# The opening and the hand-over of a fused attention and MLP kernel in another order: ACT's function table, the mixing matrices' loads, the first tile's transposes and scores, three loads of x

## The chip, the cores and the metric

One NeuronCore of a Trainium2 chip runs the whole program. The metric is device time in microseconds (us), the median of several runs. TensorE is called PE, its weight loads PEld, VectorE DVE, ScalarE ACT, GpSimd POOL and SyncE SP. DMAs are issued by SP and, in the opening, by ACT.

## The reference

Four batches, 12 heads, 448 positions, head size 64. Talking-heads attention, whose heads are mixed before and after the softmax, feeds an MLP with a piecewise quadratic gate:

```
scores = q @ k^T / 8                                  # per head, 448 x 448
scores = einsum('bhij,hg->bgij', scores, w_pre)       # mix the 12 heads
attn   = softmax over j of scores
attn   = einsum('bhij,hg->bgij', attn, w_post)        # mix again
x      = (attn @ v) laid out as 1792 x 768
h      = x @ w_in                                     # 768 -> 2048
g      = h where h >= 1, 0 where h <= -1, else (h + 1)^2 / 4
out    = g @ w_out                                    # 2048 -> 768
```

## The kernel before, in words

The order of the work is written out by hand: each engine runs its instructions as the program gives them. The attention has 16 tiles, four per batch (120, 120, 120 and 88 query positions). A tile's steps are:

- `load_q`, `load_k` bring q and k in. k of a batch comes in six head pairs of two heads each. In the first batch the two heads of a pair are two DMAs, one issued by SP and one by ACT (L101).
- `trans_q` (L138 to 141) and `trans_k` (L121 to 128) transpose them on PE into PSUM. ACT then writes a rounded high part (`qh`, `kh`) and DVE the remainder (`ql`, `kl`).
- `scores` (L155) makes the products of two head pairs, 12 matmuls; ACT (L160) and DVE (L164) copy the four results of each call to `ssb`.
- `load_s` (L179) reads ssb back through a DMA on SP, so that 10 positions times 12 heads stand on the partitions: a block.
- `pre` (L185) multiplies a block by `wpre`, which mixes the heads; `row_max` (L189), `exps` (L195) and `norm` (L201 to 206) make the softmax and scale `wpost`; `post` (L216, L218) mixes again; `pv` (L232) multiplies by v.

The blocks are worked off in 48 groups of three or four. In step n of the main loop SP first gets `load_s` for group n + 1. PE then runs `pre` of group n, `post` of group n - 1, and what the tables `at`, `vis2` and `vis` add (transposes, `pv`, scores of later tiles). Last comes the list `late[n]`, filled by `put(n, ...)`: other loads and stores, and near the end the splits of the MLP's operands. NG is 48 and NE is 44. Everything that SP issues stands in one queue; a DMA that must wait holds all DMAs behind it.

Each DMA reports to one of eight semaphores, DMAHW0 to DMAHW7, in turn. The ninth DMA of the program therefore waits on its issuing engine until the first has landed, and so on.

**The opening.** SP issues q of the first tile (in two halves), its half of the k loads and q of the second tile. ACT issues the other half of the k loads and then two small loads of w_pre and w_post (`wrep`, L480). ACT's function table is loaded before its first ACTIVATE (L140). `warm` (L499) issues matmuls whose results nobody reads. PSUM tiles of the tag "q" (two buffers, shared by `warm`, the first transposes of q and half of the scores) and "l" (six buffers) are used in turn.

**The hand-over to the MLP.** In steps 44 to 48 the first 512 rows of x are loaded back from DRAM in six pieces (`load_x`, L382, tile `xr`, three buffers) and split into `xh` on ACT (L390) and `xl` on DVE (L391) by `split_x`. A fourth piece can be loaded only when the first has been split. `load_w` (L353, L355) loads the MLP's weights and `split_w` (L373, L374) splits them; `ffn1` (L404) is the MLP's first matmul.

Of the kernel before, what the change touches and what calls it, by code (L numbers as in the profile page):

```python
# [9 lines left out]
F32 = mybir.dt.float32  # L10
# [4 lines left out]
AF = mybir.ActivationFunctionType  # L15
# [7 lines left out]
def tile_talking_heads_moe(  # L23
# [11 lines left out]
    nc = tc.nc  # L35
    B, H, S, D = q.shape
    NT, DM = out.shape
    DFF = w_in.shape[1]
    HP = H // 2
    HG = HP // 2  # L40
    IB = 10
    KM = IB * H
    QT = 12 * IB
    KC = 4
    KP = S // KC
    KDM = DM // 128
# [6 lines left out]
    const = ctx.enter_context(tc.tile_pool(name="const", bufs=1))  # L53
# [10 lines left out]
    ps_q = s_qk.enter_context(tc.tile_pool(name="ps_q", bufs=2, space=PSUM, side="right"))  # L64
# [8 lines left out]
    for b in range(B):  # L73
        for i0 in range(0, S, QT):
            n = min(QT, S - i0)
            tiles.append((b, i0, n, -(-n // IB)))
    blocks = []
    groups = []
# [17 lines left out]
    def load_k(b, hp, t=None):  # L96
        first = t is not None
        if t is None:
            t = qp.tile([KP, KC, 2, D], F32, tag="kraw", name="kraw", bufs=2)
        for s in range(2):  # L100
            (nc.scalar if first and s else nc.sync).dma_start(out=t[:, :, s, :], in_=k[b, 2 * hp + s].rearrange("(p r) d -> p r d", r=KC))  # L101
        kraw[b, hp] = t

    def load_q(t, gs=(0, 1)):
        b, i0, n, nb = tiles[t]
        if 0 in gs:
            qraw[t] = qp.tile([128, H, D], F32, tag="qraw", name="qraw", bufs=2)
        for g in gs:
            h = slice(g * HP, (g + 1) * HP)
            nc.sync.dma_start(out=qraw[t][:n, h], in_=q[b, h, i0:i0 + n].rearrange("h p d -> p h d"))  # L110
# [5 lines left out]
    def trans_k(b, hp):  # L116
        kt[b, hp] = [qp.tile([128, S], F32R, tag=f"k{c}{hp}", name=f"k{c}{hp}", bufs=1) for c in "hl"]
        x = kraw.pop((b, hp))
        ps = ps_l.tile([128, S], F32, tag="l", name="ps_k")
        for r in range(KC):  # L120
            nc.tensor.transpose(out=ps[:, r * KP:(r + 1) * KP], in_=x[:, r, :, :],  # L121
                                identity=ident[:KP, :KP])
        hi, lo = kt[b, hp]
        if b:
            nc.vector.tensor_copy(out=hi, in_=ps)
        else:
            nc.scalar.activation(out=hi, in_=ps, func=AF.Copy)
        nc.vector.tensor_tensor(out=lo, in0=ps, in1=hi.bitcast(F32), op=ALU.subtract)

    def trans_q(t, g):  # L130
        n = tiles[t][2]
        x = qraw[t]
        if g == 0:
            qt[t] = [qp.tile([128, HP, QT], F32R, tag=f"q{c}", name=f"q{c}") for c in "hl"]
        ps = (ps_l if t > 1 else ps_q).tile([128, HG, QT], F32, tag="l" if t > 1 else "q", name="ps_t")
        for m in range(HG):
            h = 2 * (g * HG + m)
            nc.tensor.transpose(out=ps[:, m, :n], in_=x[:n, h:h + 2, :], identity=ident[:n, :n])  # L138
        hi, lo = (x[:, g * HG:(g + 1) * HG, :n] for x in qt[t])
        nc.scalar.activation(out=hi, in_=ps[:, :, :n], func=AF.Copy)  # L140
        nc.vector.tensor_tensor(out=lo, in0=ps[:, :, :n], in1=hi.bitcast(F32), op=ALU.subtract)

    def scores(t, hps):

        b, i0, n, nb = tiles[t]
        if hps[0] == 0:
            ssb[t] = sp.tile([QT, H, S], F32, tag="ssb", name="ssb")
        todo = []
        rest = []
        for u, hp in enumerate(hps):  # L150
            ps = [(ps_l if u else ps_q).tile([QT, S], F32, tag="l" if u else "q", name=f"ps_s{s}")
                  for s in range(2)]
            for m, (x, y) in enumerate(((0, 0), (1, 0), (0, 1))):
                for s, r in enumerate(half):
                    nc.tensor.matmul(out=ps[s][:n], lhsT=qt[t][x][r, hp, :n], rhs=kt[b, hp][y][r, :],  # L155
                                     start=(m == 0), stop=(m == 2))
            (rest if u else todo).append((2 * hp, ps[0]))
            rest.append((2 * hp + 1, ps[1]))
        for h, x in todo:
            nc.scalar.activation(out=ssb[t][:n, h, :], in_=x[:n], func=AF.Copy)  # L160

        def copies():
            for h, x in rest:
                nc.vector.tensor_copy(out=ssb[t][:n, h, :], in_=x[:n])  # L164
        return copies
# [9 lines left out]
    def load_s(m):  # L175
        t, o, ni, c = blocks[m]
        n, nb = tiles[t][2:]
        x = ap_.tile([KM, S], F32, tag="s10", name="s10", bufs=8)
        nc.sync.dma_start(out=x[:ni * H], in_=ssb[t][o:n:nb])  # L179
        s10[m] = x  # L180
# [168 lines left out]
    def load_w(f):  # L349
        if f not in wraw:  # L350
            alloc_w(f)
        wi, wo = wraw[f]
        nc.sync.dma_start(out=wi, in_=wid[f])  # L353
        if f < NWO:
            nc.sync.dma_start(out=wo, in_=wod[f])  # L355
# [23 lines left out]
    def load_x(j, kk):  # L379
        t0, n = bat[j]  # L380
        x = pool['fp'].tile([128, TB], F32, tag="xr", name="xr", bufs=3)
        nc.sync.dma_start(out=x[:, :n], in_=xd[:, kk, t0:t0 + n])  # L382
        xraw[j, kk] = x

    def split_x(j, kk):
        n = bat[j][1]
        hi = pool['fp'].tile([128, TB], F32R, tag="xh", name="xh", bufs=KDM + 2)
        lo = pool['fp'].tile([128, TB], F32R, tag="xl", name="xl", bufs=KDM + 2)
        src = xraw.pop((j, kk))[:, :n]
        nc.scalar.activation(out=hi[:, :n], in_=src, func=AF.Copy)  # L390
        nc.vector.tensor_tensor(out=lo[:, :n], in0=src, in1=hi[:, :n].bitcast(F32), op=ALU.subtract)  # L391
        xs[j, kk] = (hi, lo)
# [65 lines left out]


    with tc.manual_schedule():  # L460
        load_q(0, (0,))
        k0 = [ap_.tile([KP, 2, KC, 2, D], F32, tag=f"v{g}", name=f"k0{g}", bufs=1) for g in range(3)]
        load_k(0, 0, k0[0][:, 0])
        load_q(0, (1,))
        for hp in range(1, HP):
            load_k(0, hp, k0[hp // 2][:, hp % 2])
        load_q(1)
        ident = const.tile([128, 128], F32, name="ident")
        make_identity(nc, ident)

# [3 lines left out]
                                base=0, pattern=[[-H, IB]], channel_multiplier=1)  # L474
        nc.gpsimd.affine_select(out=mask, in_=mask, compare_op=ALU.is_ge, fill=0.0,
                                base=H - 1, pattern=[[H, IB]], channel_multiplier=-1)
        wrep = const.tile([128, 2, H], F32, name="wrep")
        nc.vector.memset(wrep, 0.0)
        for n, w in enumerate((w_pre, w_post)):
            nc.scalar.dma_start(out=wrep[:KM, n, :], in_=w.unsqueeze(0).to_broadcast([IB, H, H]))  # L480

        wpre = const.tile([128, 128], F32, name="wpre")
        wpost = const.tile([128, H, IB], F32, name="wpost")
# [3 lines left out]
            out=wpre[:, :KM].rearrange("p (i g) -> p i g", g=H),  # L487
# [2 lines left out]
        nc.vector.tensor_tensor(  # L490
            out=wpost, in0=wrep[:, 1, :].unsqueeze(2).to_broadcast([128, H, IB]),
            in1=mask.unsqueeze(1).to_broadcast([128, H, IB]), op=ALU.mult)
        c05 = const.tile([128, 1], F32, name="c05")
        nc.vector.memset(c05, 0.5)

        def warm(n):
            ps = ps_q.tile([128, 128], F32, tag="q", name="ps_w")
            for m in range(n):
                nc.tensor.matmul(out=ps, lhsT=ident, rhs=ident, start=True, stop=True)  # L499

        warm(10)
        trans_q(0, 0)
        trans_k(0, 0)
        trans_q(0, 1)
        for hp in range(1, HP):
            warm(3)
            trans_k(0, hp)
            if hp in (3, 5):
                warm(2)
                scores(0, [hp - 3, hp - 2])()  # L510
        warm(4)
        scores(0, [4, 5])()
        for m in groups[0]:
            load_s(m)
        load_q(2)
        trans_q(1, 0)
        trans_q(1, 1)
# [4 lines left out]
        def put(n, f):  # L522
            late.setdefault(n, []).append(f)
# [18 lines left out]
        for t in range(len(tiles)):  # L542
            for g in range(3):
                w0 = 3 * t + 4 + g if t + 1 < len(tiles) else NG + 1
# [8 lines left out]
        NE = NG - 4  # L553
        for j in range(3):
            put(NE, lambda j=j: load_x(0, j))
        put(NE, lambda: load_w(0))
        for kk in range(KDM):
            put(NE + 1 + kk // 2, lambda kk=kk: split_x(0, kk))
            if kk + 3 < KDM:
                put(NE + 1 + kk // 2, lambda kk=kk: load_x(0, kk + 3))  # L560
        for f in range(1, NWE):
            put(NE + f, lambda f=f: load_w(f))
        put(NG - 1, lambda: split_w(0))
# [6 lines left out]
        for n in range(NG + 2):  # L570
            if n == NE:
# [4 lines left out]
                    name="ps_h", bufs=2, space=PSUM, side="right", reuse_waits="tile"))  # L576
# [29 lines left out]
            for f in [scores(t, hps) for t, hps in vis.pop(n, ())]:  # L606
                f()
# [79 lines left out]
```

## Time and profile before

| What | Value |
|---|---|
| median of three runs | 975.99 us (975.35 to 978.43) |
| the profiled execution, its own time | 973.09 us |
| its span | 971.4 us |
| PE busy | 947.6 us, 98% of the span |
| DVE, ACT, POOL busy | 57%, 53%, 17% |

The profile belongs to one execution. Its times count from the span's start; 1.7 us of its own time lie around the span. A row of the timeline gives start, length, engine, line, operation, `out<-in`, count, and in brackets the idle time of that engine before it with what ended it. An engine's name with a q (ACTq, SPq) is its sequencer issuing a DMA: the length is that of issuing, not of the transfer. An fp32 matmul is recorded as two PE entries, so ten `warm` matmuls are 20 entries.

### The profile page before, as it was taken

How to read it: one execution, taken by the hardware profiler on the slowest of the kernel's cores; microseconds unless marked ns; L12 is line 12 of the kernel's file. 1: busy time of each engine (PE TensorE's matmuls, PEld its weight loads, DVE VectorE, ACT ScalarE, POOL GpSimd, SP SyncE). 2: the span in 40 equal slices, each digit the busy share in tenths (PEclk: the TensorE clock that was granted, in tenths of full speed). 3: DMA queues.
4: the chain of work that ended last, by engine and by line, in shares of the span. 5: the costliest groups of instructions: out<-in, count | busy, mean ns of one | idle time of the engine just before them, and what ended most of it. 6: DMA issues, size and time to landing. Idle time of an engine off the chain costs nothing.

```text
span 971.4 us, 17796 instructions
## 1 busy us (share of the span) xinstructions
PE 947.6 (98%) x6698; PEld 775.7 (80%) x6698; DVE 554.7 (57%) x997; ACT 517.9 (53%) x1097; POOL 169.2 (17%) x253
## 2 busy tenths in 40 slices
PE   7999999999999999999899999999999999999997
PEld 6667777777778787777688877888888888888997
DVE  3665756666665756654355566554454644545774
ACT  2566577666676666665555454443333533334553
POOL 0134233323333233422201212000000000000000
PEclk8999999999999999999999999999999999999999
DMA  5685657775667856653544432020000200000100
GB/s 88 177 240 163 198 177 216 212 211 176 198 199 218 218 173 206 191 196 107 166 163 140 149 128 87 11 98 1 1 23 1 92 1 1 12 1 6 65 2 33
DMA packets 118362, 115.22 MB, mean 119 GB/s; under 512 B 61700, under 2 KB 107268, under 8 KB 118276
## 3 DMA queue, kind: packets, MB, share of 16 engines
q1 hardware_dynamic: 115232, 113.37, 38.4%
q10 hardware_dynamic: 3044, 0.70, 0.5%
q8 instruction: 54, 0.88, 0.4%
q14 instruction: 32, 0.26, 0.1%
HBM read 55.85 MB, written 19.66 MB: 78 GB/s over the span
## 4 chain that ended last, share of the span: by engine, by line
PE 91%; DMA 3%; DVE 2%; ACT 1%; issue 1%; POOL 1%; ACTq 0%; SPq 0%; POOLq 0%
PE o L441 22%; PE ps_h L404 22%; PE ps_l L185 15%; PE ps_a L216 15%; PE ps_x L232 8%; PE ps_s L155 7%; DMA s<-ssb 2%; PE ps_w L499 1%; PE ps_k L121 1%; PE ps_t L138 1%; POOL wo L286 1%; DMA k<-in_k_dram 1%; DMA wi<-wid 0%; DVE mx L418 0%; DVE mx L417 0%
## 5 line engine op out<-in xcount | busy, mean ns | idle before, releaser
L216 PEld LDWEIGHTS ps_a<-wr,e 128*112 128x112 f32 x1440 | 154.6, 177 | 18.5 <-issue 18.5
L195 ACT ACTIVATE e<-ps_l,nm 128x448 f32<-128x448 f32 x180 | 113.0, 632 | 94.3 <-DVE nm L189 93.7
L206 POOL TENSOR_SCALAR wr<-wpost,rs 128x120 f32<-128x120 f32 x180 | 103.2, 591 | 337.1 <-DVE rs L202 290.4
L185 PE MATMUL ps_l<-s,wpre 120*128 120x448 f32 x360 | 150.3, 559 | 6.6 <-DMA s<-ssb 6.6
L216 PE MATMUL ps_a<-wr,e 128*112 128x120 f32 (+1 forms) x1440 | 155.3, 266 | 0.0
L404 PE MATMUL ps_h<-xh,wil 128*128 128x512 f32 (+1 forms) x384 | 139.5, 363 | 0.0
L404 PE MATMUL ps_h<-xl,wih 128*128 128x512 f32 (+1 forms) x384 | 139.2, 363 | 0.0
L404 PE MATMUL ps_h<-xh,wih 128*128 128x512 f32 (+1 forms) x384 | 139.2, 362 | 0.0
L185 PEld LDWEIGHTS ps_l<-s,wpre 120*128 120x128 f32 x360 | 64.6, 191 | 72.2 <-issue 62.0
L441 PE MATMUL o<-woh,gl 128*128 128x512 f32 x448 | 115.7, 339 | 4.4 <-DVE gl L421 4.4
L189 DVE TENSOR_REDUCE nm<-ps_l 128x1 f32<-128x448 f32 x180 | 105.1, 618 | 21.1 <-PE ps_l L185 16.0
L441 PE MATMUL o<-woh,gh 128*128 128x512 f32 x448 | 115.6, 339 | 0.0
L441 PE MATMUL o<-wol,gh 128*128 128x512 f32 x448 | 115.2, 339 | 0.0
L417 DVE TENSOR_TENSOR mx<-ps_h,a 128x512 f32<-128x512 f32 (+1 forms) x64 | 39.9, 624 | 120.6 <-ACT a L416 120.6
L164 DVE COPY ssb<-ps_s 120x448 f32<-120x448 f32 (+1 forms) x144 | 82.6, 619 | 44.3 <-PE ps_s L155 41.4
L416 ACT ACTIVATE a<-ps_h,c 128x512 f32<-128x512 f32 (+1 forms) x64 | 40.5, 633 | 113.5 <-PE ps_h L404 113.4
L218 ACT ACTIVATE aT<-ps_a 112x480 f32<-112x480 f32 x180 | 96.0, 591 | 4.9 <-PE ps_a L216 3.6
L441 PEld LDWEIGHTS o<-woh,gl 128*128 128x128 f32 x448 | 75.1, 189 | 17.9 <-DVE gl L421 6.8
L420 ACT ACTIVATE gh<-mx 128x512 fp32r<-128x512 f32 (+1 forms) x64 | 37.0, 578 | 92.5 <-DVE mx L418 92.5
L441 PEld LDWEIGHTS o<-wol,gh 128*128 128x128 f32 x448 | 76.3, 188 | 10.0
L441 PEld LDWEIGHTS o<-woh,gh 128*128 128x128 f32 x448 | 76.4, 188 | 9.7
L232 PE MATMUL ps_x<-aT,v 112*64 112x120 f32 (+1 forms) x1536 | 83.8, 262 | 0.0
(66 smaller groups left out, 1246.5 us busy)
## 6 DMA issues: line engine op xcount, KB each, us to landing
s<-ssb SPq DMA_DIRECT2D x172, 210.0 KB
wraw<-in_moe_w_in_dram SPq DMA_DIRECT2D x32, 384.0 KB
raw<-in_moe_w_out_dram SPq DMA_DIRECT2D x20, 384.0 KB
wid<-wt SPq DMA_DIRECT2D x32, 192.0 KB
wi<-wid SPq DMA_DIRECT2D x16, 384.0 KB
v<-in_v_dram SPq DMA_DIRECT2D x12, 448.0 KB
out_dram<-osb SPq DMA_DIRECT2D x14, 384.0 KB
wraw<-in_moe_w_out_dram SPq DMA_DIRECT2D x12, 384.0 KB
```

What stands on the lines that cost most here:

```text
L155: nc.tensor.matmul(out=ps[s][:n], lhsT=qt[t][x][r, hp, :n], rhs=kt[b, hp][y][r, :], start=(m == 0), stop=(m == 2))
L164: nc.vector.tensor_copy(out=ssb[t][:n, h, :], in_=x[:n])
L185: nc.tensor.matmul(out=lps[m], lhsT=wpre[:k], rhs=s10.pop(m)[:k], start=True, stop=True)
L189: nc.vector.tensor_reduce(out=nm, in_=lps[m], axis=AX.X, op=ALU.max, negate=True)
L195: nc.scalar.activation(out=e, in_=ps, func=AF.Exp, bias=nm, accum_out=sm[:, j:j + 1])
L206: nc.gpsimd.tensor_scalar_mul(out=w[:, :, :ni], in0=wpost[:, :, :ni], scalar1=rs[:, j:j + 1])
L216: nc.tensor.matmul(out=ps[:, r, :ni * H], lhsT=e[:, r * KP:(r + 1) * KP], rhs=w[:, :, :ni], start=True, stop=True)
L218: nc.scalar.activation(out=aT[t][:, :, :, c:c + ni], in_=ps[:, :, :ni * H].rearrange("q r (h i) -> q r h i", h=H), func=AF.Copy)
L232: nc.tensor.matmul(out=ps[s * D:(s + 1) * D, m, :n], lhsT=vt[b, g][:, 2 * m + s, r * D:(r + 1) * D], rhs=a[:, r, 4 * g + 2 * m + s, :n], s ...
L404: nc.tensor.matmul(out=ps[:, :n], lhsT=w[:, kk, :], rhs=x[:, :n], start=(c == 0), stop=(c == last))
L416: nc.scalar.activation(out=a[:, :n], in_=ps[:, :n], func=AF.Relu, scale=0.5, bias=c05)
L441: nc.tensor.matmul(out=o[bank][:, c0:c0 + ne], lhsT=g[:, t * 128:(t + 1) * 128], rhs=w[:, e0:e0 + ne], start=(f == 0 and m == 0 and c0 == ...
```

## The change

At the start ACT first runs one ACTIVATE on a constant, which brings its table load to the head of its queue. Of the first batch's k loads SP issues both halves of head pairs 0 to 2, ACT both halves of pairs 3 to 5. The two `wrep` loads go from ACT's queue to the end of SP's. The scores of the first tile come after all its transposes, with two `warm` matmuls ahead of each head pair's transposes instead of three, and none ahead of the scores (36 in all instead of 49). Of the first tile's score copies ACT takes two of each four, not one. `wpre` and `wpost` are built on DVE behind those copies. In the hand-over `load_x` of pieces 3 and 4 stands in step 46, not 45, that of piece 5 in step 47, not 46, and piece 3 is split in step 47, not 46.

```diff
@@ load_k
         for s in range(2):
-            (nc.scalar if first and s else nc.sync).dma_start(out=t[:, :, s, :], in_=k[b, 2 * hp + s].rearrange("(p r) d -> p r d", r=KC))
+            (nc.scalar if first and hp > 2 else nc.sync).dma_start(out=t[:, :, s, :], in_=k[b, 2 * hp + s].rearrange("(p r) d -> p r d", r=KC))
@@ scores
-            (rest if u else todo).append((2 * hp, ps[0]))
+            (rest if u and t else todo).append((2 * hp, ps[0]))
@@ the opening
     with tc.manual_schedule():
+        c05 = const.tile([128, 1], F32, name="c05")
+        nc.vector.memset(c05, 0.5)
         load_q(0, (0,))
+        c1 = const.tile([128, 1], F32, name="c1")
+        nc.scalar.activation(out=c1, in_=c05, func=AF.Copy)
...
         load_q(1)
+        wrep = const.tile([128, 2, H], F32, name="wrep")
+        nc.vector.memset(wrep, 0.0)
+        for n, w in enumerate((w_pre, w_post)):
+            nc.sync.dma_start(out=wrep[:KM, n, :], in_=w.unsqueeze(0).to_broadcast([IB, H, H]))
...
-        wrep = const.tile([128, 2, H], F32, name="wrep")
-        nc.vector.memset(wrep, 0.0)
-        for n, w in enumerate((w_pre, w_post)):
-            nc.scalar.dma_start(out=wrep[:KM, n, :], in_=w.unsqueeze(0).to_broadcast([IB, H, H]))
...
+        warm(10)
+        trans_q(0, 0)
+        trans_k(0, 0)
+        trans_q(0, 1)
+        for hp in range(1, HP):
+            warm(2)
+            trans_k(0, hp)
+        for g in range(3):
+            scores(0, [2 * g, 2 * g + 1])()
+        for m in groups[0]:
+            load_s(m)
...
-        c05 = const.tile([128, 1], F32, name="c05")
-        nc.vector.memset(c05, 0.5)
...
-        warm(10)
-        trans_q(0, 0)
-        trans_k(0, 0)
-        trans_q(0, 1)
-        for hp in range(1, HP):
-            warm(3)
-            trans_k(0, hp)
-            if hp in (3, 5):
-                warm(2)
-                scores(0, [hp - 3, hp - 2])()
-        warm(4)
-        scores(0, [4, 5])()
-        for m in groups[0]:
-            load_s(m)
@@ the hand-over
-        for kk in range(KDM):
-            put(NE + 1 + kk // 2, lambda kk=kk: split_x(0, kk))
-            if kk + 3 < KDM:
-                put(NE + 1 + kk // 2, lambda kk=kk: load_x(0, kk + 3))
+        for w0, loads, splits in ((1, (), (0, 1)), (2, (3, 4), (2,)), (3, (5,), (3, 4, 5))):
+            for kk in loads:
+                put(NE + w0, lambda kk=kk: load_x(0, kk))
+            for kk in splits:
+                put(NE + w0, lambda kk=kk: split_x(0, kk))
```

On ACT, at the head of its queue, before (k_82, k_83 and k_84 hold head pairs 0 and 1, 2 and 3, 4 and 5; the brackets name what the row waits for):

```order
L101 DMA k_82<-in_k_dram 112x4x64 x2
L101 DMA k_83<-in_k_dram 112x4x64 x2
L101 DMA k_84<-in_k_dram 112x4x64 [waits DMAHW0_49]
L101 DMA k_84<-in_k_dram 112x4x64 [waits DMAHW2_49]
L480 DMA wrep<-in_w_pre_dram 120x1x12 [waits DMAHW4_49,DVE_49]
L480 DMA wrep<-in_w_post_dram 120x1x12 [waits DMAHW5_49]
L140 ACT_TABLE_LOAD
L140 ACTIVATE qh<-ps_t 128x360 [waits PE_49]
L127 ACTIVATE kh_140<-ps_k 128x448 [waits PE_49]
```

and the same place with the change (k_87 holds pairs 2 and 3, k_88 pairs 4 and 5):

```order
L465 ACT_TABLE_LOAD
L465 ACTIVATE c_84<-c_80 128x1 [waits DVE_49]
L101 DMA k_87<-in_k_dram 112x4x64 x2
L101 DMA k_88<-in_k_dram 112x4x64
L101 DMA k_88<-in_k_dram 112x4x64 [waits DMAHW0_49]
L101 DMA k_88<-in_k_dram 112x4x64 [waits DMAHW2_49]
L101 DMA k_88<-in_k_dram 112x4x64 [waits DMAHW4_49]
L140 ACTIVATE qh<-ps_t 128x360 [waits PE_49]
L127 ACTIVATE kh_137<-ps_k 128x448 [waits PE_49]
```

The table load stands ahead of the DMAs instead of behind them, eight DMAs have become six, and three of them wait for an earlier DMA to land: the last for the second load of head pair 3.

On SP, at the hand-over (`s` is what load_s writes, three rows a group: 46 first, then 47), before:

```order
L382 DMA xr<-xd 128x512 x3
L353 DMA wi_5857<-wid 128x768
L355 DMA wo_5858<-wod 128x768
L179 DMA s_5861<-ssb 120x1x448
L179 DMA s_5863<-ssb 120x1x448
L179 DMA s_5865<-ssb 120x1x448
L382 DMA xr<-xd 128x512 x2
L353 DMA wi_5949<-wid 128x768
L355 DMA wo_5950<-wod 128x768
L179 DMA s_5953<-ssb 120x1x448
L179 DMA s_5955<-ssb 108x1x448
L179 DMA s_5957<-ssb 108x1x448
```

and with the change, from the first load of group 46 on:

```order
L179 DMA s_5847<-ssb 120x1x448
L179 DMA s_5849<-ssb 120x1x448
L179 DMA s_5851<-ssb 120x1x448
L353 DMA wi_5931<-wid 128x768
L355 DMA wo_5932<-wod 128x768
L179 DMA s_5935<-ssb 120x1x448
L179 DMA s_5937<-ssb 108x1x448
L179 DMA s_5939<-ssb 108x1x448
L248 DMA xd<-xo 768x1x120
L382 DMA xr<-xd 128x512 x2
L353 DMA wi_6016<-wid 128x768
L355 DMA wo_6017<-wod 128x768
```

The two loads of x that wait for a split stood ahead of the loads of group 47 and now stand behind them; the weight loads `wi` and `wo` of the second slice still stand ahead.

## Rows read from the trace of the kernel before

**Rows 1.** The page's busy times of the engines, then one row of PE's waits over the whole span (engine, line waited for: us in total, times, longest us).

```profile
PE 947.6 (98%) x6698; PEld 775.7 (80%) x6698; DVE 554.7 (57%) x997; ACT 517.9 (53%) x1097; POOL 169.2 (17%) x253
...
PE ps_l L185 <- DMA s<-ssb: 6.6, 3, 4.3
```

**Rows 2.** The timeline of ACT and its queue in the opening.

```profile
0.78 6.26 ACTq L101 DMA_DIRECT2D k<-in_k_dram  x6
...
9.41 0.80 ACTq L480 DMA_DIRECT2D wrep<-in_w_post_dram  x1
10.23 1.28 ACT L140 ACT_TABLE_LOAD   x1 [10.23 <-DMA k<-in_k_dram]
11.53 0.47 ACT L140 ACTIVATE qh<-ps_t 128x360 fp32r<-128x360 f32 x1
```

**Rows 3.** Single k loads on ACT's queue: the second one's issue (chain of waits: start, length, what), then the fifth and the sixth, which wait until the first and the second have landed (timeline of short stretches).

```profile
1.53 0.64 ACTq L101
...
4.51 0.57 ACTq L101 DMA_DIRECT2D k<-in_k_dram  x1
...
6.47 0.57 ACTq L101 DMA_DIRECT2D k<-in_k_dram  x1
```

**Rows 4.** The timeline of PE in the opening: the transposes of q's second half, and the first `warm` behind them.

```profile
7.62 0.50 PE L138 MATMUL ps_t<-ident,qraw 120*128 120x120 f32 x3 [0.65 <-DMA qraw<-in_q_dram]
...
12.84 1.65 PE L499 MATMUL ps_w<-ident 128*128 128x128 f32 x6 [4.71 <-DVE ql L141]
```

**Rows 5.** Stretches of the opening: length, busy us and instructions of PE, PEld, DVE, ACT, POOL, granted clock of PE (1.00 is 2.4 GHz, 0.50 is 1.2 GHz), busy share of the DMA engines, GB/s.

```profile
4.00:6.00 2.00, 2.00 (x11) 2.00 (x11) 0.00 (x0) 0.00 (x0) 0.00 (x0) 1.00 1.12 215
...
8.00:10.00 2.00, 0.12 (x2) 0.00 (x0) 0.00 (x0) 0.00 (x0) 0.00 (x0) 0.96 1.24 170
...
12.00:14.00 2.00, 1.16 (x5) 1.16 (x6) 1.71 (x5) 0.80 (x2) 0.00 (x0) 0.50 0.99 192
...
16.00:18.00 2.00, 2.00 (x18) 2.00 (x18) 0.82 (x2) 0.54 (x1) 0.00 (x0) 0.84 0.00 0
```

**Rows 6.** The chain of waits in the opening (start, length, what, PE entries): transposes and three `warm` at the lower clock, the same at the full clock, one call of scores, the last `warm`, the first `pre`.

```profile
14.49 0.75 PE ps_k L121 x4
15.23 1.31 PE ps_w L499 x6
...
18.57 1.55 PE ps_s L155 x12
...
20.98 0.38 PE ps_k L121 x4
21.37 0.68 PE ps_w L499 x6
...
28.67 3.84 PE ps_w L499 x32
32.51 3.10 PE ps_l L185 x8
```

**Rows 7.** The timeline from the last copies of the first tile's scores to PE's wait near 58 us.

```profile
26.49 1.69 DVE L164 COPY ssb<-ps_s 120x448 f32<-120x448 f32 x3 [0.95 <-PE ps_s L155]
28.10 0.96 DVE L141 TENSOR_TENSOR ql<-ps_t,qh 128x360 fp32r<-128x360 f32 x2
28.27 3.47 SPq L179 DMA_DIRECT2D s<-ssb  x4
...
35.59 0.30 PEld L138 LDWEIGHTS ps_t<-ident,qraw 120*128 120x128 f32 x3 [0.71 <-DMA qraw<-in_q_dram]
...
58.12 1.88 PE L185 MATMUL ps_l<-s,wpre 120*128 120x448 f32 x4 [2.00 <-DMA s<-ssb]
```

**Rows 8.** The timeline of SP's queue at the hand-over.

```profile
456.57 2.92 SPq L179 DMA_DIRECT2D s<-ssb  x3
...
467.81 0.92 SPq L382 DMA_DIRECT2D xr<-xd  x2
...
469.78 2.82 SPq L179 DMA_DIRECT2D s<-ssb  x3
...
474.52 0.33 SPq L382 DMA_DIRECT2D xr<-xd  x1
```

**Rows 9.** PE at the hand-over: `pre` of group 46 and of group 47 in the chain of waits, and the latter in the timeline, with the idle time before it.

```profile
466.12 2.45 PE ps_l L185 x6
...
477.14 4.19 PE ps_l L185 x6
...
477.14 4.19 PE L185 MATMUL ps_l<-s,wpre 120*128 120x448 f32 x6 [4.32 <-DMA s<-ssb]
```

**Rows 10.** Two stretches of the hand-over, columns as in rows 5.

```profile
458.00:462.00 4.00, 4.00 (x29) 2.71 (x26) 1.88 (x3) 2.02 (x6) 0.51 (x1) 1.00 0.86 255
462.00:466.00 4.00, 4.00 (x55) 3.77 (x53) 0.34 (x2) 2.62 (x6) 1.70 (x3) 1.00 0.41 132
```

**Rows 11.** The timeline of the splits at the hand-over and of the first matmul that needs them.

```profile
473.14 1.14 ACT L390 ACTIVATE xh<-xr 128x512 fp32r<-128x512 f32 x2
...
486.55 1.29 DVE L391 TENSOR_TENSOR xl<-xr,xh 128x512 fp32r<-128x512 f32 x2 [3.26 <-ACT xh L390]
...
487.80 0.96 DVE L374 SCALAR_TENSOR_TENSOR wil<-wi,wih 128x768 fp32r<-128x768 f32 x1
...
489.87 0.50 PE L404 MATMUL ps_h<-xh,wil 128*128 128x512 f32 x1
```

More of the change, by code (lines that the diff above doesn't have):

```diff
@@ L476, in tile_talking_heads_moe, with warm @@
                                 base=H - 1, pattern=[[H, IB]], channel_multiplier=-1)
-        wrep = const.tile([128, 2, H], F32, name="wrep")
-        nc.vector.memset(wrep, 0.0)
-        for n, w in enumerate((w_pre, w_post)):
-            nc.scalar.dma_start(out=wrep[:KM, n, :], in_=w.unsqueeze(0).to_broadcast([IB, H, H]))
+        def warm(n):
+            ps = ps_q.tile([128, 128], F32, tag="q", name="ps_w")
+            for m in range(n):
+                nc.tensor.matmul(out=ps, lhsT=ident, rhs=ident, start=True, stop=True)
+        warm(10)
[9 more added lines that the diff above has]
+            load_s(m)
         wpre = const.tile([128, 128], F32, name="wpre")
@@ L492, in tile_talking_heads_moe @@
             in1=mask.unsqueeze(1).to_broadcast([128, H, IB]), op=ALU.mult)
-        c05 = const.tile([128, 1], F32, name="c05")
-        nc.vector.memset(c05, 0.5)
[L496 to L499, printed above, removed]
-        warm(10)
-        trans_q(0, 0)
-        trans_k(0, 0)
-        trans_q(0, 1)
-        for hp in range(1, HP):
-            warm(3)
-            trans_k(0, hp)
-            if hp in (3, 5):
-                warm(2)
-                scores(0, [hp - 3, hp - 2])()
-        warm(4)
-        scores(0, [4, 5])()
-        for m in groups[0]:
-            load_s(m)
         load_q(2)
```

## The prediction

> **What bounds the kernel now.** I read the page first: PE is busy for 947.6 of 971.4 us, so only its idle time and its slow stretches can be won, and of the waits over the whole span the longest is one of 4.3 us for a load of `s` [rows 1]. Then the timeline of the opening, engine by engine. ACT issues DMAs until 10.21 (9.41 and 0.80) and only then loads its table for 1.28 us; its first useful ACTIVATE starts at 11.53 [rows 2]. PE has done q's transposes by 8.12 and stands until 12.84, since the `warm` next in its queue reuses the PSUM buffer that ACT and DVE have yet to read [rows 4]. During that idle time the granted clock falls to 0.50 (1.2 GHz); it returns to 1.00 (2.4 GHz) in the stretch from 16 to 18, after some 4 us of work [rows 5]. From there PE runs the first tile's transposes and scores, and the first `load_s` is issued at 28.27, when DVE's last copy is done [rows 7]. Last the hand-over: SP issues the loads of group 46 from 456.57 to 459.49, then stands until 467.81, because the fourth piece of x needs a buffer that a split must free; the loads of group 47 stand behind it and go out at 469.78 [rows 8]. PE wants them 4.32 us before they land, and its clock falls on top: that `pre` takes 4.19 us where the one before took 2.45 [rows 9].
>
> **The opening, step by step.** With the table load at the head, ACT begins its DMAs at about 2.4 (0.78 + 1.28 and a short ACTIVATE). Three go at once at 0.6 to 0.7 us each. The last of six waits until the second load of head pair 3 has landed, which was issued near 3.1. In the old order the first load on this queue had landed 3.7 us after its issue (0.78 to 4.51) and the second 4.9 us after (1.53 to 6.47) [rows 2, 3]; so ACT is free between 7.4 and 8.6, instead of 11.53. I take 8.3. From ACT's first ACTIVATE to PE's next `warm` it was 1.3 us (11.53 to 12.84) [rows 2, 4]: PE goes on at 9.6, some 3 us earlier.
>
> The loads then set the pace. q of the first tile is two loads of 120 x 6 x 64 floats (0.37 MB), k twelve of 112 x 4 x 64 (1.38 MB). The opening moved 170 to 215 GB/s with both queues at work, and 192 with SP alone from 12 to 14, where the second tile's q (0.37 MB, 1.9 us at that rate) was the last thing to land [rows 5]. Where that q stays behind every k load, k is complete near 12 at the latest and near 11 at best. Pair 2's second half is the last k load on SP, pair 5's on ACT, and I take 11.7 for both. PE waits for pair 2, then has four pairs' transposes in a row: pair 2's own, and three times two `warm` and a transpose. At the lower clock these are 0.75 and three times 1.62 (two thirds of 1.31, and 0.75), at the full clock 0.38 and three times 0.83 [rows 6]. The first scores therefore start between 13.9 and 17.6; I take 16.2, with the clock returning on the way.
>
> Three calls of scores at 1.55 us [rows 6] with short waits for the two shared buffers (I allow 0.15 each, since ACT and DVE now have two copies of 0.56 apiece per call) make 5.1, and the last copy 0.7: `load_s` at 16.2 + 5.9 = 22.1, which is 6.2 us earlier than 28.27 [rows 7]. PE gains a little less. Its last `warm` waits for the second tile's `ql`, and on DVE `wpre` and `wpost` now stand in between: three short instructions, each shorter than one `ql` (0.48 [rows 7]), 0.7 us together. Copies to 22.0, these to 22.7, `ql` to 23.2: the `warm` starts there and no longer at 28.67, 5.4 us earlier [rows 6]. After that PE waits less for transfers, which are 6.2 ahead: the 0.71 us for q and the 2.00 us near 58 shrink [rows 7]. **The opening is worth 5.6 us**, between 4.2 (scores from 17.6) and 7.9 (from 13.9).
>
> The rest of the opening I cost at nothing. The `wrep` loads on SP are some 12 KB behind q and land near 14, 8 us before DVE reads them; were they later, every us beyond that would hold DVE, and the `warm` and `pre` behind it. The second tile's q stays behind the k loads and is needed after the scores. Thirteen fewer `warm` are counted in the sums above.
>
> **The hand-over.** With the change the two loads of x that wait stand behind the loads of group 47. After group 46's loads end at 459.49 SP can issue `wi` and `wo` of the second slice and then group 47's `s` at once, as far as earlier DMAs have landed: near 460.5 to 463. Ahead of them then lie what was still moving until 465 and 0.79 MB of weights. The DMA engines moved 255 GB/s from 458 to 462 and were well below that from 462 to 466 [rows 10]; weights and `s` (0.6 MB) need 1.4 MB / 0.25 = 5.6 us after 465, so the first block lands near 469 and the last near 471. PE ends its work ahead of `pre` at 472.8 (477.14 less 4.32), so the wait goes: 4.32, and the clock stays up: 4.19 - 2.45 = 1.74 [rows 9]. The pieces of x come no later in time, only in program order: pieces 3 and 4 can be issued when the first two splits are done, at about 467.8 as before, and piece 5 when piece 2 is split, near 474.5 as before [rows 8, 11]. What is added is one more split in front of the weights' split: 0.57 us on ACT, 0.65 on DVE (halves of 1.14 and 1.29). `wil` was done at 488.76 and wanted at 489.87 [rows 11], so 1.1 us of cover stand against 0.65; without the cover it would cost 0.65 at most. **The hand-over is worth 6.0 us**, between 3 (if the block lands 3 us into the old wait) and 6.1.
>
> **Sum.** 5.6 + 6.0 = 11.6 us. The profiled execution took 973.09, which gives 961.5. The median shown is 975.99, 2.9 above it: 964.4 on that scale. The likely ends are 14.0 (962.0) and 7.2 (968.8).
>
> **A rule against the change.** The clock came back in the stretch from 16 to 18 while PE ran three `warm` and four transposes in turn [rows 5, 6]; the change leaves two `warm` a pair. The Trainium skill, page "TensorE: Matmul & The Clock Gate", section "Part 4: PE-mode transpose", says that transposes do not count as busy work for that clock the way matmuls do. By that rule alone the thinner mix would stay at 1.2 GHz longer, which is the first rival; the row shows only that a mix with more `warm` did return to 2.4 GHz.
>
> **The rivals.**
> - *The clock stays at half through the transposes and the first call of scores.* Scores then start at 17.6, 1.4 us later than I take, and the first call takes 1.55 us more, so the opening is worth 2.6: 967.4. For it: PE waits for k twice in this stretch. Against: the idle pieces are shorter than the 4.7 us in which it fell before [rows 4].
> - *Group 47's loads are still late*, behind the weights and group 46's own: 3 us of the 6 remain as a wait and a fallen clock: 967.4. For it: the DMA engines are at 0.86 and 255 GB/s at that time. Against: 132 GB/s in the next stretch leaves room [rows 10].
> - *The change does not bring the order in time that it has in the program*: ACT's queue starts later than SP's, the load of pair 3 that its last issue waits for lands near 11, and SP still holds group 47 behind a landing. The opening is then worth 1 or 2 and the hand-over nothing: within 3 us of before.
> - *Slower: PE stays at 1.2 GHz past the first group.* Its place is the stretch from the first scores on. Each us of full-clock PE work costs one more: 4.65 for the scores, 3.84 for the last `warm`, 3.1 for the first `pre` [rows 6], 11.6 together, which is all the gain. The point that decides is whether the clock is still at half when the first `pre` ends; if it lasts through the next group (some 8 us of PE work), the run takes about 984. Against it: in the same scores, with waits between the calls, the clock was 1.00 from about 17 on [rows 5].
>
> **How the numbers follow.** Chances: the forecast 0.65, the clock through the transposes 0.16, group 47 still late 0.10, hardly any effect 0.05, slower 0.04. About 0.3%, 3 us, is what a measurement of this kernel can tell from no change. The first three are all faster by more than that: 0.91; same 0.05; slower 0.04. The range takes in the forecast's ends and the next two cases, with 1 us more at either side for the spread of the runs: 960.5 to 969.5.
>
> **What would show it.** Right: one table load before 1 us, the first `qh` near 8, PE at work again by 10, scores from about 16 in three calls without a break, the first `load_s` near 22, the last `warm` near 23; at the hand-over no wait before `pre` of group 47, each of its matmuls at the length of group 46's, and `ffn1` starting some 12 us earlier than 489.87 with no new wait for `wil`. Wrong: `qh` past 10; transposes at 0.75 us beyond 16; a DMA wait before that `pre`; or a new wait in `ffn1`, or a longer one near 58, that takes the gain back.

## The result, and the profile of the changed kernel

The changed kernel takes **961.55 us** (960.54 to 963.55, four runs), the kernel before, run beside it, 976.48 (975.35 to 978.43): a ratio of 0.9848 [0.9824, 0.9871], or 14.9 us. Forecast were 964.4 and 11.6 us. The two profiled executions are closer together: 963.55 is the longest of the changed kernel's four, 973.09 is shorter than the four timed runs of before beside it, so between the two traces (spans of 971.4 and 961.8) only 9.6 us can be followed.

ACT and its queue in the opening; it answers to [rows 2].

```profile
0.78 1.28 ACT L465 ACT_TABLE_LOAD   x1 [0.78 <-PEq L671]
0.95 1.36 ACTq L101 DMA_DIRECT2D k<-in_k_dram  x2
...
2.34 4.22 ACTq L101 DMA_DIRECT2D k<-in_k_dram  x4
...
6.68 0.47 ACT L140 ACTIVATE qh<-ps_t 128x360 fp32r<-128x360 f32 x1 [4.41 <-PE ps_t L138]
```

The table load is over at 2.06, and two DMAs were issued while it ran. ACT has issued its last at 6.56, 3.7 us before the old 10.21, and `qh` begins 4.85 us earlier than it did.

PE: from the second half of q to the first scores, the last `warm`, a `pre` at full clock, the `pre` near 54 and the `post` behind it, then the hand-over's `pre` of groups 46 and 47 and the first `ffn1` [rows 4, 6, 7, 9, 11].

```profile
8.28 0.50 PE L138 MATMUL ps_t<-ident,qraw 120*128 120x120 f32 x3 [1.13 <-DMA qraw<-in_q_dram]
8.62 0.62 PE L489 MATMUL ps_w<-ident 128*128 128x128 f32 x4
10.33 1.01 PE L121 MATMUL ps_k<-ident,k 112*128 112x112 f32 x4 [1.10 <-DMA k<-in_k_dram]
11.13 1.09 PE L489 MATMUL ps_w<-ident 128*128 128x128 f32 x4
...
16.93 0.55 PE L121 MATMUL ps_k<-ident,k 112*128 112x112 f32 x4
17.41 0.46 PE L155 MATMUL ps_s<-kh,qh 64*120 64x448 f32 x2
...
24.25 3.84 PE L489 MATMUL ps_w<-ident 128*128 128x128 f32 x32 [1.12 <-DVE ql L141]
...
43.64 3.27 PE L185 MATMUL ps_l<-s,wpre 120*128 120x448 f32 x8
...
53.57 4.94 PE L185 MATMUL ps_l<-s,wpre 120*128 120x448 f32 x8 [1.97 <-DMA s<-ssb]
58.35 3.45 PE L216 MATMUL ps_a<-wr,e 128*112 128x120 f32 x32
...
462.47 2.52 PE L185 MATMUL ps_l<-s,wpre 120*128 120x448 f32 x6
...
469.17 2.52 PE L185 MATMUL ps_l<-s,wpre 120*128 120x448 f32 x6
...
480.24 0.50 PE L404 MATMUL ps_h<-xh,wil 128*128 128x512 f32 x1
```

The old wait of 4.71 us has become two of 1.13 and 1.10, for q and for k. From 10.33 on PE waits for nothing, but its pieces have the lower clock's lengths (transposes 1.01, two `warm` 1.09, for 0.55 and 0.62 later), so the scores start at 17.41. The last `warm` starts 4.4 us earlier than before. At 53.57 a wait of 1.97 remains, and the `pre` behind it takes 4.94 us, where at full clock the same four matmuls (eight entries) took 3.27 at 43.64. The `post` after it starts at 58.35; before it started at 61.99 (row below): of 4.4 us 3.6 are left. At the hand-over both `pre` take 2.52 without a wait; `ffn1` starts 9.63 us earlier than at 489.87.

```profile
61.99 3.45 PE L216 MATMUL ps_a<-wr,e 128*112 128x120 f32 x32
```

Stretches of the changed kernel, columns as in [rows 5].

```profile
8.00:10.00 2.00, 0.95 (x7) 0.79 (x7) 0.92 (x2) 0.47 (x1) 0.00 (x0) 0.99 1.33 206
10.00:12.00 2.00, 1.67 (x8) 1.60 (x8) 0.05 (x1) 0.54 (x1) 0.00 (x0) 0.50 1.24 189
...
14.00:16.00 2.00, 2.00 (x12) 2.00 (x12) 0.98 (x2) 0.54 (x1) 0.00 (x0) 0.50 0.00 0
16.00:18.00 2.00, 2.00 (x16) 1.82 (x17) 0.62 (x1) 1.03 (x2) 0.00 (x0) 0.80 0.00 0
...
54.00:56.00 2.00, 2.00 (x5) 0.95 (x4) 0.62 (x1) 0.58 (x2) 0.00 (x0) 0.58 0.65 243
```

PE was busy for half of the stretch from 8 to 10, then the clock is 0.50 until near 16.8 (0.80 over the stretch from 16 to 18), and it is low again around 55. All k had landed by 14 (no DMA traffic behind it): from there it is the clock, not a load, that holds the transposes.

SP's queue: the first tile's `load_s`, and the hand-over [rows 7, 8].

```profile
23.09 3.29 SPq L179 DMA_DIRECT2D s<-ssb  x4
...
453.29 3.02 SPq L179 DMA_DIRECT2D s<-ssb  x3
456.36 0.61 SPq L353 DMA_DIRECT2D wi<-wid  x1
457.02 0.47 SPq L355 DMA_DIRECT2D wo<-wod  x1
457.59 3.06 SPq L179 DMA_DIRECT2D s<-ssb  x3
...
464.23 1.26 SPq L382 DMA_DIRECT2D xr<-xd  x2
```

Group 47's loads follow group 46's by 4.3 us instead of 13.2. The pieces of x are issued behind them, and neither PE nor ACT waits for them there.

### The profile page after: what moved, and what is told of

Its sections match the earlier page's. It is cut to its first block, busy times and chain, and to the rows that moved or that the text cites. A ratio compares the mean times of both kernels' runs of the same rounds, so it can differ in the third digit from the quotient of the medians.

```text
span 961.8 us, 17743 instructions
## 1 busy us (share of the span) xinstructions
PE 945.2 (98%) x6672; PEld 773.8 (80%) x6672; DVE 553.1 (58%) x994; ACT 519.7 (54%) x1101; POOL 169.4 (18%) x253
## 4 chain that ended last, share of the span: by engine, by line
PE 83%; issue 5%; DVE 4%; ACT 2%; POOL 1%; DMA 1%; POOLq 0%; ACTq 0%; SPq 0%; DVEq 0%
PE o L441 20%; PE ps_h L404 18%; PE ps_l L185 15%; PE ps_a L216 15%; PE ps_x L232 8%; PE ps_s L155 6%; POOL wo L286 1%; DMA s<-ssb 1%; PE ps_t L138 1%; PE ps_k L121 1%; DVE mx L418 1%; DVE mx L417 1%; ACT wih L373 1%; ACT gh L420 1%; DVE wil L374 1%
```

## Experiments

Each ratio is against runs of before made beside it; "us" is (ratio - 1) x 976. The rows come from several chips, so rows are compared by their ratios.

| Kernel | median us (runs) | ratio [95%] | us |
|---|---|---|---|
| changed | 961.55 (4) | 0.9848 [0.9824, 0.9871] | -14.8 |
| changed, again | 961.25 (4) | 0.9858 [0.9836, 0.9879] | -13.9 |
| hand-over alone | 967.36 (5) | 0.9915 [0.9899, 0.9930] | -8.3 |
| opening alone | 966.79 (6) | 0.9910 [0.9894, 0.9927] | -8.8 |
| before, six `xr` buffers | 968.95 (6) | 0.9932 [0.9914, 0.9950] | -6.6 |
| ACT's queue alone | 977.49 (12) | 1.0022 [1.0006, 1.0039] | +2.1 |
| the same, `wpre` and `wpost` late | 966.95 (6) | 0.9907 [0.9879, 0.9935] | -9.1 |
| new order alone | 972.08 (12) | 0.9960 [0.9943, 0.9978] | -3.9 |
| changed, old k halves | 957.35 (6) | 0.9813 [0.9785, 0.9840] | -18.3 |
| changed, more `warm` | 959.12 (4) | 0.9825 [0.9808, 0.9842] | -17.1 |
| the same, v later | 958.13 (5) | 0.9821 [0.9799, 0.9843] | -17.5 |
| changed, old k halves, v later | 955.58 (5) | 0.9801 [0.9780, 0.9821] | -19.4 |
| before, again | 976.30 (10) | 1.0013 [0.9997, 1.0029] | +1.3 |

**1. Hand-over alone**: before, with the new loop for `load_x` and `split_x`.

> The kernel before with the hand-over's loads of x in the changed order and nothing else. My account (the gain is two separate parts, hand-over 6.0 us by removing one 4.32 us wait and 1.74 us at the lower clock): 6.0 us below the kernel before, so about 970.5 when that stands at 976.5; no wait before the pre of group 47 and its six entries 2.45 us long. Rival (the two parts depend on each other: the loads come in time only because the opening is early): under 3 us, above 973.5. Rival (the timed runs hold more at the hand-over than the profiled one): 8 us or more, under 968.5.

Measured -8.3. The wait before `pre` of group 47 is gone:

```profile
472.36 2.52 PE L185 MATMUL ps_l<-s,wpre 120*128 120x448 f32 x6
```

The trace is 5.8 us under that of before (span 965.6 for 971.4), close to the 6.0 of the account. The medians show more, and by them it is the second rival that came (8 us or more). That timed runs of before can hold more at the hand-over is seen in one other trace (experiment 10); for the rest it is not shown.

**2. Opening alone**: the changed kernel with the old loop.

> The changed kernel with the hand-over's loops of the kernel before. My account: the opening alone is worth 3.6 us in the two profiles (PE's first post behind the wait near 58 us starts 3.6 us earlier) and at most 5.6: 971 to 973. If the measured 14.9 us of the whole change is 6 for the hand-over and the rest for the opening: 9 us, about 967.5.

Measured -8.8, with the wait at the hand-over back:

```profile
473.76 4.19 PE L185 MATMUL ps_l<-s,wpre 120*128 120x448 f32 x6 [4.26 <-DMA s<-ssb]
```

The account taken from the two profiles (3.6, at most 5.6) missed; the 9 us read off the medians came. This run's trace, its longest execution of six, is only 3.3 us under that of before (968.1 for 971.4). The two parts add up to 17.1 against 14.8 for the whole. With intervals of 1.5, 1.6 and 2.3 us to either side that is not a proven difference.

**3. Six `xr` buffers**, so that no load of x waits for a split, with the old order in SP's queue.

```diff
-tag="xr", name="xr", bufs=3
+tag="xr", name="xr", bufs=6
```

> The kernel before with six buffers for the loaded pieces of x instead of three, so that no load of x waits for a split; program order as before. If SP's standing behind the split is the cause of the late loads of group 47: the wait of 4.3 us before that pre goes, and the run is about 6 us below the kernel before (970.5), with SP issuing group 47 before 465. If the cause is the DMA engines' load instead (1.3 MB of x and weights ahead of it): the wait stays above 3 us and the time within 2 us of before.

PE's wait in this kernel:

```profile
PE ps_l L185 <- DMA s<-ssb: 3.2, 4, 1.6
```

Without moving a DMA the longest wait, the one before `pre` of group 47, falls from 4.3 to 1.6, and -6.6 us follow; SP issues that group's loads at 461.76 instead of 469.78. So it was SP standing behind a split that held group 47, as the prediction has it; 1.6 us of wait remain with the two loads of x still ahead of the rows.

**4. ACT's queue alone**: before, with the table load at the head and `wrep` on SP; `wpre` and `wpost` stay where they were on DVE.

> The kernel before with the table load at the head of ACT's queue and the wrep loads on SP, and nothing else: k halves, transposes, scores and the hand-over as before. If ACT's late start is what the opening loses: qh starts near 7.2 instead of 11.53 and the first load_s is issued 3 to 4.5 us earlier than 28.27; the run is 3 to 6 us below the kernel before. If the loads of k and the lower clock set the pace: under 2 us earlier and under 2 us gained.

A miss. ACT is free as forecast (`qh` at 7.32), but PE waits longer than before. PE, then DVE:

```profile
15.20 1.65 PE L501 MATMUL ps_w<-ident 128*128 128x128 f32 x6 [7.03 <-DVE ql L141]
```

```profile
14.22 0.28 DVE L490 SCALAR_TENSOR_TENSOR wpre<-mask,wrep 128x120 f32<-128x120 f32 x1 [13.11 <-DMA wrep<-in_w_pre_dram]
14.42 0.28 DVE L494 TENSOR_TENSOR wpost<-wrep,mask 128x120 f32<-128x120 f32 x1
14.61 0.53 DVE L141 TENSOR_TENSOR ql<-ps_t,qh 128x360 fp32r<-128x360 f32 x1
```

`ql` stands behind `wpre`, and `wrep`, now last in SP's queue, lands near 14.2. The wait has moved from ACT to DVE, and the first `load_s` goes out at 31.23, 3 us later than before.

**5. The same with `wpre` and `wpost` late**: their three DVE instructions behind the first tile's copies, and nothing else new (old scores, old `warm`, old k halves).

> The kernel before with the table load at the head of ACT's queue and `wrep` on SP, as in the run of ACT's queue alone, and with the three DVE instructions that build `wpre` and `wpost` moved behind the first tile's score copies (warm counts, scores and k halves as before). Theory (in that run DVE stood before `ql` for `wrep`, and this alone ate the gain): `qh` near 7.3 again, PE's next `warm` near 8.6 and not 15.20, the first `load_s` near 24.5 (28.27 before, less the 3 to 4 us that PE begins earlier), no wait of PE over 3 us in the opening; the time 3 to 4 us under before. Rival (the lower clock or the k loads take the gain in any case): restart near 8.6, but `load_s` within 1 us of 28.27 and the time within 1.5 us of before.

PE in this kernel:

```profile
8.14 0.94 PE L490 MATMUL ps_w<-ident 128*128 128x128 f32 x6 [0.21 <-DVE ql L141]
8.91 0.55 PE L121 MATMUL ps_k<-ident,k 112*128 112x112 f32 x4
...
22.88 3.84 PE L490 MATMUL ps_w<-ident 128*128 128x128 f32 x32 [1.57 <-DVE ql L141]
```

PE goes on at 8.14 and the clock never falls in the opening (transposes at 0.55). The first `load_s` goes out at 21.73 (24.5 expected), the last `warm` is at 22.88, earlier than in the changed kernel, and -9.1 us are as much as the whole opening is worth (-8.8). It is more than either theory gave.

**6. New order alone**: transposes first, then scores, two `warm`, `wpre` late; ACT's queue, k halves and hand-over as before.

> The kernel before with the first tile's transposes ahead of all its scores, two warm matmuls a pair, ACT's share of the copies and wpre behind them; table load, wrep loads, k halves and the hand-over as before. qh starts at 11.5 as before. Two warm and a transpose take 1.62 us at the lower clock and 0.83 at the full one, so scores start near 18.6 and load_s goes out near 24.5: 3.5 us earlier, 3 to 5 us gained. If the order alone is worth nothing (the transposes only move): load_s after 27 and under 1 us.

Measured -3.9: `qh` is at 11.58 as forecast, the first `load_s` at 25.73 (2.5 us earlier), scores at 20.01 and not 18.6, since PE ran at 1.2 GHz until near 18.8. Queue and order add up to 13.0, but the opening alone has 8.8. The two need not add, and the intervals (2.7 us to either side for the queue) leave it open; the one part that neither run has is the split of k, which the next experiment takes out.

**7. Old k halves** in the changed kernel, and the changed kernel again, beside experiment 11 on one chip, as a control.

```diff
-(nc.scalar if first and hp > 2 else nc.sync).dma_start(out=t[:, :, s, :],
+(nc.scalar if first and s else nc.sync).dma_start(out=t[:, :, s, :],
```

> The changed kernel with the k loads split between SP and ACT as before (one head of each pair on each queue). Theory (the lower clock, not the k loads, sets when the first scores start): `qh` near 7.3 instead of 6.68, scores within 0.7 us of 17.41, time within 1 us of the changed kernel's 961.5. Rival (the split brings the pairs earlier, and is worth something by itself): PE waits for `k` 2 us or more in all in the transposes, scores past 18.5, time 1.5 us or more above 961.5.

> The changed kernel as it is, once more, beside the version with old k halves on one chip. If the split of the k loads is what holds the clock down from 10 to 17: 960.5 to 963.5 as before, some 4 us above the version with old halves, clock .995 to .998 in every run, and in the profile PE's wait for `k` near 9 to 10 us with 1.2 GHz behind it. Rival (the two calls ran on different chips and that is the difference): the two within 1.5 us of each other, or the clock at 1.000.

PE with the old halves, then two stretches, then PE in the changed kernel's second profile:

```profile
7.70 0.50 PE L138 MATMUL ps_t<-ident,qraw 120*128 120x120 f32 x3 [0.87 <-DMA qraw<-in_q_dram]
8.34 0.71 PE L489 MATMUL ps_w<-ident 128*128 128x128 f32 x4
8.89 0.55 PE L121 MATMUL ps_k<-ident,k 112*128 112x112 f32 x4
...
13.30 0.46 PE L155 MATMUL ps_s<-kh,qh 64*120 64x448 f32 x2
...
20.14 3.84 PE L489 MATMUL ps_w<-ident 128*128 128x128 f32 x32 [1.12 <-DVE ql L141]
```

```profile
8.00:10.00 2.00, 1.86 (x17) 1.66 (x16) 1.27 (x3) 1.15 (x3) 0.00 (x0) 1.00 1.33 205
10.00:12.00 2.00, 1.83 (x16) 1.51 (x15) 1.26 (x3) 1.10 (x3) 0.00 (x0) 1.00 1.27 187
```

```profile
8.40 0.83 PE L138 MATMUL ps_t<-ident,qraw 120*128 120x120 f32 x3 [1.38 <-DMA qraw<-in_q_dram]
9.02 1.07 PE L489 MATMUL ps_w<-ident 128*128 128x128 f32 x4
10.38 1.01 PE L121 MATMUL ps_k<-ident,k 112*128 112x112 f32 x4 [0.28 <-DMA k<-in_k_dram]
```

Both theories of this run missed. With one head of each pair on either queue, pair 1 is transposed at 8.89 instead of 10.33, the clock stays at 1.00, the scores start at 13.30 and the last `warm` is at 20.14: 4.1 us earlier than in the changed kernel. The medians say 957.35 for 961.55 and 961.25, but the intervals of the ratios overlap a little. What decides is the chip on which the changed kernel ran again beside experiment 11, which has the old halves: clock .996 to .998 against .999 to 1.000 in all runs, and the last `warm`, first in the changed kernel and then with the old halves, 3.4 us apart:

```profile
23.38 3.84 PE L489 MATMUL ps_w<-ident 128*128 128x128 f32 x32 [1.12 <-DVE ql L141]
...
19.98 3.84 PE L489 MATMUL ps_w<-ident 128*128 128x128 f32 x32 [1.12 <-DVE ql L141]
```

So the chip is not the cause; the later v of experiment 11 is issued only from 44.38 on. In the changed kernel's second profile the time and the clock came as expected, but the wait for k ahead of pair 1 is only 0.28, and the clock is down before it, already in q's second half: SP now issues both heads of pair 0 ahead of that half (at 2.73 us, formerly at 2.08), and both of pair 1 behind it. The change's own split of k thus costs 3.4 to 4.1 us of the opening.

**8. More `warm`** in the changed kernel, to fill its waits in the opening.

```diff
         trans_k(0, 0)
+        warm(4)
         trans_q(0, 1)
...
-            warm(2)
+            warm(7 if hp == 1 else 2)
```

> The changed kernel with 4 more warm matmuls ahead of the second transposes of q and 7 instead of 2 ahead of head pair 1, in the time in which PE waited for q (1.1 us) and k (1.1 us). If the lower clock from 10 to 16.4 us (transposes 0.95, two warm 1.09 per pair instead of 0.55 and 0.62) is what made the first scores start at 17.4: the clock stays at 1.00 through the opening, scores start near 14, and the run is 2.5 to 3.5 us below the changed kernel. If the loads of k set the pace: scores start after 16.5 and the gain is under 1 us.

The clock is at 1.000 in all four runs, the scores start at 15.49 (near 14 expected), the last `warm` at 22.34, and the median is 2.4 us under the changed kernel's, just short of the 2.5 expected. k is still late (0.79 us for pair 2). The last `warm` is 1.9 us earlier than in the changed kernel and 2.2 later than with the old halves: about half of the cost went through the clock, the rest through the late loads and the nine added matmuls, which this run does not tell apart.

**9. The same, v later**: each load of v in step 2 + g, not all in step 1, where they stand in SP's queue ahead of rows that PE wants near 53.

```diff
-            put(1, lambda g=g: load_v(0, g))
+            put(2 + g, lambda g=g: load_v(0, g))
```

> The changed kernel with the extra warm matmuls (4 and 7) and the first batch's three loads of v put into steps 2, 3 and 4 instead of all into step 1, so that 1.4 MB stand no longer ahead of the third group's loads of s. If those loads cause PE's waits near 50 us (0.9 us with the extra warm, 2.0 in the changed kernel): no wait there and 0.5 to 1 us below the run with the extra warm alone (958 to 958.7). If the wait is only pushed on to a later group: 959 to 960.

No wait for `s` is left anywhere, as expected; 958.13 is within the runs' spread of the row above, and by the ratios a gain in time is not shown.

**10. Before, again**, for the spread of its runs.

> The kernel before, unchanged, for a second profiled execution. The first took 973.09 and ran at a mean granted clock of 0.993; its other executions took 973.8 to 978.8 at 0.988 to 0.992. My account: the difference is time at 1.2 GHz after PE's waits, so a slower execution shows the same waits and a longer or further stretch at 0.50 (near 58 us or near 477 us), some 3.4 us of it costing 1.7. Rival: the difference is spread over the run (longer instructions or waits elsewhere); then the granted clock by stretches is as in the first profile.

Ten runs and the 29 beside them go from 972.51 to 978.79 and roughly follow the mean granted clock: of the 29, five at .995 take 972.7 to 973.6, five at .987 or .988 take 977.5 to 978.4 (the shortest of all is at .992). The hand-over in this profile:

```profile
476.00:478.00 2.00, 0.79 (x1) 0.50 (x2) 0.00 (x0) 0.00 (x0) 0.00 (x0) 0.72 1.06 261
478.00:480.00 2.00, 2.00 (x4) 0.96 (x3) 0.62 (x1) 0.20 (x1) 0.00 (x0) 0.50 0.91 308
480.00:482.00 2.00, 2.00 (x4) 0.82 (x3) 0.62 (x1) 1.25 (x4) 0.00 (x0) 0.50 0.28 105
482.00:484.00 2.00, 2.00 (x14) 2.00 (x13) 0.97 (x3) 1.06 (x3) 0.00 (x0) 0.57 0.01 5
```

After a wait of 4.77 us PE runs at 1.2 GHz until near 483.7. In the first profile, after 4.32, it was back at 2.4 GHz before 481. That `pre` starts only 0.07 us later than in the first profile, the first `pv` behind it 1.58 later (485.30 for 483.72), and the spans differ by 1.6: the whole difference of the two lies there. One wait, then, has a price that differs from run to run, by 3 us of slow stretch here.

**11. Old k halves and v later**, the best that the runs above point to.

> The changed kernel with the old k halves, as in the run before, and each load of v in step 2 + g instead of all in step 1, as in the best version so far. Theory (what spreads the times of the version with old halves, 955.9 to 959.6, is the wait of PE for `s` near 50 us, which comes and goes with the loads of v ahead in SP's queue): 955.5 to 957, spread under 1.5 us, granted clock 1.000 in all runs. Rival (the spread has another source, or the later v is itself waited for in `pv`): 957 to 958.5 with the same spread of 3 to 4 us, or a new wait of PE for `v`.

955.58 us with all five runs within 0.2, clock .999 to 1.000, no wait for `s`, `ffn1` at 472.27: it beats the kernel before by 19.4 us and the changed one by 5.7 (961.25 on the same chip). That the wait for `s` is what spread the runs of experiment 7 fits this, but the one trace of that kernel has no such wait.

## Why the prediction was right, and where its sum was not

The sign, the places and the mechanisms held. The time was 2.9 us under the forecast, within its range, and terms were off in both directions: on the traces the gain was 2.0 us smaller than the sum, on the medians larger. That the two partly cancel is luck.

- **Hand-over, 6.0 us forecast.** `ffn1` starts 9.63 us earlier and `pre` of group 46 was 3.58 earlier already (466.05 in the timeline of before): 6.05 come from the hand-over. Both reasons were seen: the wait went, and `pre` kept its full-clock length. No wait for `wil` came in their place.
- **Opening, 5.6 us forecast (4.2 at least); 3.6 in the traces.** ACT was free at 6.56, not 8.3, since it issues while its table loads; PE went on at 8.62, not 9.6. The step that failed is the next, "the loads then set the pace": PE never waited for pair 2. It waited for q's second half and for pair 1, ran at 1.2 GHz until near 16.8, and the scores came at 17.41 for 16.2. That is the first rival as far as the transposes go, and the argument against it failed: idle pieces of 1.13 and 1.10 us, far shorter than 4.7, were enough for the clock to fall. The first call of scores ran at full clock, which spared the rest of its price.
- **The split of k had no price in the sum.** Counting the DMAs ahead of q's second half and of pair 1 on SP would have pointed to it: one more and two more. It cost 3.4 to 4.1 us (experiment 7).
- **"The rest of the opening I cost at nothing" was true of the whole and hid its condition.** `wrep` lands near 14.2 in experiment 4, and near 14 was forecast. But it is harmless only because `wpre` and `wpost` stand behind the copies: without that the gain of ACT's queue is lost (+2.1 for -9.1, experiments 4 and 5).
- **The wait near 58** was to shrink; it is still 1.97 (0.49 in the second profile), and the clock now fell behind it, 1.67 us. That gave back 0.8 us of the opening's gain (4.4 us at the last `warm`, 3.6 at that `post`).
- **The scale.** On traces the forecast was 961.5 for 963.55: 2.0 too good, all of it in the opening (`ffn1`, some 12 us earlier by forecast, came 9.63 earlier). The medians differ by 5.3 us more than the traces. The runs of before beside the experiments have a median clock of .990 to .992, the profiled one .993, the changed kernel's runs .995 to .998. A thousandth is worth some 0.7 us (experiment 10: 4.8 us for seven), so some 5 thousandths between the medians are 3.5 us, against 1.4 between the two traces. A sum over one profiled run could not show that its wait costs more in others. But the hand-over's wait is not all of it: experiment 2 still has that wait, and gains 3.3 us in its trace and 8.8 by the medians. The other 3 us of the 5.3 are not traced; runs of before differ by as much.
- **The rule on transposes.** With two `warm` a pair PE worked from 10.33 to near 16.8 at 1.2 GHz, and in experiment 6 from 12.67 to near 18.8; with three, before, from 12.84 to near 16.6. The Trainium skill says ("TensorE: Matmul & The Clock Gate", "Part 4: PE-mode transpose") that transposes do not count as busy work for the clock in the same way. These rows agree in direction, but do not prove it: experiment 4, with three, was down from its restart at 15.20 to near 20.4, and the second profile of the changed kernel, with two, from before 8.4 only to near 14.9.

## What to carry to other kernels

When an instruction's input is moved to the end of a queue, look at what stands behind that instruction on its own engine: the load may cost nothing at its new place while the instruction, left at its old one, stalls all that follows it. In an opening fed by two queues, count how many transfers stand ahead of the very first ones that are needed, since balance over the whole set says nothing of the first pair. Where PE waits for some us, price the slow stretch behind the wait from several runs, and look for gains in removing the wait rather than shortening the work.

## What the runs showed of the hardware

- ACT's sequencer issued two DMAs (0.95 to 2.31) while the table load ran (0.78 to 2.06).
- After waits of 4.3 and 4.8 us at one place the granted clock was low until before 481 in one run and until near 483.7 in another; the kernel without such waits (experiment 11) had runs within 0.2 us of each other, the kernel before (experiment 10) within 6.3.
- The rows show a granted clock of 1.00 from 4 to 6, yet twenty `warm` entries of the changed kernel's start took 4.64 us (0.23 each), and 32 at full clock took 3.84 (0.12 each). The six of 1.31 us at 1.2 GHz in [rows 6] have 0.22 each: in these first microseconds the lengths are those of 1.2 GHz, whatever the column says.
